# One core, Trainium2: the output product's first two loads issued 16 steps sooner, odd blocks' norms in later steps, the last pair's splits farther apart

## The chip, the cores and the metric

The kernel runs on one core of a Trainium2 chip. The metric is the time of one execution on the device, in microseconds (us), as the median of several runs.

## The reference

Attention in chunks gives `x` of 3072 tokens by 512; two mixtures follow it, each a small feed-forward net, with a norm between them:

```python
def _moe_ref(x, w_in, w_out):                 # 512 -> 2048 -> 512
    h = x @ w_in
    sp = np.where(h > 20.0, h, np.log1p(np.exp(np.minimum(h, 20.0))))
    g = h * np.tanh(sp)
    return (g @ w_out).astype(np.float32)

def _moe2_ref(x, w_gate, w_val, w_out, rms_g):  # 512 -> 1536 -> 512
    rms = np.sqrt(np.mean(x * x, axis=-1, keepdims=True) + 1e-06)
    xn = x / rms * rms_g
    g = xn @ w_gate
    silu = g * (1.0 / (1.0 + np.exp(-g)))
    val = xn @ w_val
    return (silu * val @ w_out).astype(np.float32)

x = attn_out.transpose(0, 2, 1, 3).reshape(3072, 512)
return _moe2_ref(_moe_ref(x, ...), ...)
```

## The kernel before, in words

All matrix work is done on TensorE (PE) in a split form: each fp32 operand is kept as hi + lo, and a product is three matmuls, hi by hi, hi by lo and lo by hi (`L639` to `L641` in `product`, `L754` to `L756` in `mm3`). The split is made by `split` (`L151` to `L154`): ScalarE (ACT) casts hi (`L153`), VectorE (DVE) subtracts to get lo (`L154`). POOL is GpSimd, SP is SyncE, which issues nearly all DMAs.

The stages in order of time:

- Attention, with the first products of the first mixture in its gaps, to about 300 us.
- `group1`: `x` by `w_in`, in groups of seven products (`group`, `L643` to `L670`) in place of eight. ScalarE copies a bank out (`L649`, `L657`), VectorE adds the rest (`L654`, `L665`, `L668`, `L670`). The result `g` goes to DRAM (`g_scratch`). The last pass, `group1(3, ...)`, ends at about 378 us.
- The output product of the first mixture, `out1`, 48 steps `(m, i)`: six blocks `m` of 512 tokens, eight steps `i` in each; a step is 24 matmuls. The class `Feed` loads the operand of a step from `g_scratch` (`L771`), applies mish (`L782`) and splits it. Three steps are prepared by `feeding` during the last group of the first mixture; later ones three to five steps ahead. This is the stage from about 378 to 640 us.
- The norm of a block, `rms_pieces`, is cut into pieces that wait in a list, `pend`; after a step of the next block a number of them, given by a tuple by `i`, are taken off and issued. Piece `p1` splits the sum of squares and adds it over the partitions with two matmuls by ones (`L833`); `p2` loads ScalarE's tables and takes the root by `Ln` and `Exp` (`L839` to `L841`). After an odd block the seven operands of the block pair are formed and split in the same way and stored to `nt_scratch`; a pair's seven operands are later loaded by `t_load` (`L628`), in the order 1, 6, 5, 4, 2, 7, 3.
- `group2`: the gated stage, for three pairs `j`, forwards and then backwards, from about 640 to 985 us. The last pair's operands are split while pair 0 is worked on: `both` puts the pieces in `pend`, an `x` of a string is a piece and a dot is an empty slot, and `between2` takes one off in each gap between products. When `pend` is empty `between2` goes on with the conversion of the weights (`L149` loads them raw, `L202` to `L216` convert).
- `group3`: the second output product, to the end.

The order of instructions is not that of the code alone. The program is given in the code's order and a scheduler then orders each engine's list, with the code's order as priority. So each engine works off a fixed list and stands where an instruction of it waits, with all behind it.

Of the kernel before, what the change touches and what calls it, by code (L numbers as in the profile page):

```python
# [29 lines left out]
def tile_kernel(  # L30
# [76 lines left out]
    def flush(all_=False):  # L107
        tick[0] += 1
        while late and (all_ or late[0][0] <= tick[0]):
            _, dst, src = late.pop(0)  # L110
            nc.sync.dma_start(out=dst, in_=src)


    def w_slot(u):
        pool = w1p if u < NW1 else w2p[0]
        return pool.tile([128, SLOT], F32R, tag=f"w{u}", name="w")
# [3 lines left out]
    def as7(s):  # L120
        return s.rearrange("p (a l f) -> p a l f", a=7, l=2)

    def w_load(key, u, cuts=((0, 7),)):
        s = w_slot(u)
        for a, b in cuts:
            at = slice(512 * a, 512 * b)
            nc.sync.dma_start(out=s[:, at].bitcast(F32), in_=wd[key][:, at].bitcast(F32))
        wtab[key] = as7(s)
# [180 lines left out]
    def cv_upto(n):  # L309
        while cv_n[0] < n:  # L310
            next(cv[0], None)
            cv_n[0] += 1
# [231 lines left out]
    def att_list(j):  # L544

        out = []
        t0 = TPP * j
        for s in range(TPP + 4):
            for op, lag in (("e", 4), ("d", 3), ("c", 2), ("b", 1), ("a", 0)):
                t = t0 + s - lag  # L550
                if t0 <= t < t0 + TPP:
                    if op == "a" and t % SPB == 0:
                        out.append([(att_a0, t)])
                    out.append([(att_ops[op], t), (att_ops[op + "1"], t)])
        return out
# [10 lines left out]
    def t_new2():  # L566
        return late_pools["t"].tile([128, 2, 2, N2], F32R, tag="T", name="T")
# [131 lines left out]
    def run(parts, between):  # L699
        while parts:  # L700
            for part in list(parts):
                if next(part, "end") == "end":
                    parts.remove(part)
                else:
                    between()
# [8 lines left out]
    def group1(j, i, between):  # L714
        run([group1_parts(j, i)], between)

    def group1_parts(j, i):
        need(("i", i))
        g = [gp.tile([128, 2, N], F32, tag="g", name="g") for _ in range(2)]
        ts = {p: ttab_x[j, p] for p in ORDER}  # L720
        at = W_AT if i < 3 else W_IN
        mul = lambda p, bank_, first: product(at[p], wtab["i", i], ts[p], bank_, first)
        banks = group_banks(4)
        c11 = banks[0][:, 0:N]
        temps = lambda: [cp.tile([128, N], F32, tag="c", name="c") for _ in range(3)]
        yield from group(mul, banks, N, g[0][:, 1, :], g[1][:, 0, :], g[1][:, 1, :], temps)
        nc.scalar.copy(g[0][:, 0, :], c11)
        for e in range(2):
            store_later(
                g_d[2 * i + e, :, 2 * N * j:2 * N * j + 2 * N].rearrange("p (a n) -> p a n", a=2),  # L730
                g[e],
            )
# [205 lines left out]
    down = up[::-1]  # L938
# [51 lines left out]
    def slots(pieces, conv, tail=(), more={}, cap=10 ** 6):  # L990


        state = dict(n=0, att=0, tail=0)
        plist, n_slots = pieces
        first_cv, to = conv
        base = cv_n[0]

        def between():
            state["n"] += 1
            n = state["n"]  # L1000
            flush()
            if n in more:
                more[n]()
            span = n_slots - 7
            while state["att"] < len(plist) and state["att"] * span < n * len(plist):
                for fn, t in plist[state["att"]]:
                    fn(t)
                state["att"] += 1
            if n > first_cv:
                cv_upto(min(cap, base + (to - base) * (n - first_cv) // (n_slots - first_cv)))  # L1010
            if n >= n_slots - 7 and tail:
                if state["tail"] == 0:
                    state["t"] = tail()
                    for fn in state["t"][0]:
                        fn()
                elif state["tail"] <= len(state["t"][1]):
                    state["t"][1][state["tail"] - 1]()
                state["tail"] += 1

        return between  # L1020

    def tail_of(j):
        return lambda: t_pieces(j, xb.pop(2 * j), xb.pop(2 * j + 1), t_new, lambda p: g_new(), None, ttab_x)
# [8 lines left out]
    CV_I = 64  # L1032
# [15 lines left out]
    more = {}  # L1048
    finish_at(more, 7, at[1, 7] + 1)
    bt = slots((att_list(1), 4 * len(units)), (0, 73), tail_of(1), calls(more), CV_I)  # L1050
# [4 lines left out]
    more = {}  # L1055
# [7 lines left out]
    bt = slots((att_list(2), 56), (12, CV_I + 33 + 11), tail_of(2), calls(more), CV_I + 33)  # L1063
    for i in down:
        group1(1, i, bt)
    more = {}
# [3 lines left out]
    bt = slots((att_list(3), 56), (0, 0), tail_of(3), calls(more))  # L1070
# [8 lines left out]
    w2p[0] = late_pool("w2p", 1, "right")  # L1079
    late_pools["s"] = late_pool("gs", 3, "right")  # L1080
    late_pools["gr"] = late_pool("gr", 1, "right")
    bt = slots(([], 56), (0, CV_I + 44))
    for pos, i in enumerate(down[:-1]):
        group1(3, i, bt)
        if 1 <= pos <= 3:
            back, u = ((1, 4), (2, 0), (0, 1))[pos - 1]
            w_load(("i", back), u)
    steps = [(m, i) for m in range(NB2) for i in range(F1 // 2)]

    def g_src(m, i):  # L1090
# [1 line left out]

    jorder = list(range(NPAIR2))
    feed = Feed(steps, g_src, ACTF.Mish)

    def feeding(feed, between):

        calls = [lambda: feed.load(4), lambda: None, lambda: feed.split(1), lambda: None,
                 lambda: feed.split(2), lambda: None, lambda: feed.split(3)]

        def fn():
            between()
            calls.pop(0)()

        return fn
# [8 lines left out]
    pend = []  # L1114
# [12 lines left out]
    for s, (m, i) in enumerate(steps):  # L1127
        t = feed.next(s)
        out1(m, i, t)
        flush()  # L1130
        if i == F1 // 2 - 1 and m < NB2 - 1:
            assert not pend
            p0, pend = rms_pieces(m, m, t_new2, sq_new, v_parts)
            p0()
            if m % 2:
                def both(m=m):
                    early, rest = t_pieces(m // 2, xn.pop(m - 1), xn.pop(m), t_new2, v_temp,
                                           nt_d[m // 2], {})
                    pend.extend(early + rest)
                pend.append(both)  # L1140
        elif i < F1 // 2 - 1:
            for _ in range((0, 1, 2, 2, 2, 3, 3)[i]):
                if pend:
                    pend.pop(0)()
        cv_upto(CV_I + min(64 + 78 * (s + 1) // len(steps), 44 + 4 * (s + 1)))
        n_raw[0] = 2 * (F1 // 2) + 6 + F1 + 12
        if m == NB2 - 1 and i in (1, 3, 5, 6):
            row_slots.clear()
            f, u = {1: (2, 5), 3: (3, 6), 5: (4, 3), 6: (5, 2)}[i]
            w_load(("gv", f), u)  # L1150
        if s == len(steps) - 3:
            t_load(jorder[0], nt_d[jorder[0]], ttab_n)
# [2 lines left out]
    hold = w_slot(0)  # L1155
    upper = hold[:, 4 * N2:6 * N2].bitcast(F32).rearrange("p (a n) -> p a n", a=2)

    def raw_pair():
        flush(True)
        parts = [rawp.tile([128, 512, 2], I32, tag="raw", name="raw") for _ in range(2)]  # L1160
        return tuple(
            x.rearrange("p f t -> p (f t)").bitcast(F32R).rearrange("p (a n) -> p a n", a=2)
            for x in parts
        )

    def last_temp(p):
# [5 lines left out]
    p0, pend = rms_pieces(  # L1172
        NB2 - 1, NB2 - 1,
        lambda: hold[:, 0:4 * N2].rearrange("p (a b n) -> p a b n", a=2, b=2),
        lambda: [upper[:, a] for a in range(2)], sm_parts, "1.2..rab",
    )
    p0()

    def both():
        early, rest = t_pieces(NPAIR2 - 1, xn.pop(NB2 - 2), xn.pop(NB2 - 1), raw_pair,  # L1180
                               last_temp, nt_d[NPAIR2 - 1], {})
        parts = early + rest
        pend.extend(parts.pop(0) if c == "x" else (lambda: None) for c in "x.x.x.xx.xxx")
    pend.append(both)

    def between2(to, n_slots):
        state = dict(n=0)
        base = cv_n[0]

        def fn():  # L1190
            flush()
            if pend:
                pend.pop(0)()
                return
            n_raw[0] = 10 ** 6
            state["n"] += 1
            cv_upto(min(to, base + (to - base) * state["n"] // n_slots))

        return fn

    bt = between2(CV_I + 220, 100)
    for jn, j in enumerate(jorder):
        last = jn == NPAIR2 - 1
        if jn:
# [28 lines left out]
    bt = between2(CV_I + 298, 92)  # L1233
# [54 lines left out]
```

## Time and profile before

| | before |
|---|---|
| runs, us | 1164.95, 1170.21, 1170.44 |
| median, us | 1170.21 |
| profiled execution, us | 1167.72 |
| its span, us | 1166.0 |
| mean granted clock of TensorE | 0.993 |

The profile is of one execution; its span runs from the first to the last instruction, and 1.7 us lie around it. A row of a timeline gives the start and the duration in us, the engine, the line of the code, the operation with its tiles, and in brackets how long the engine stood idle before it and what ended that. SPq is SyncE's queue of DMA issues; a row there gives the time the queue spent on issuing, not the transfer. Durations of neighbouring instructions on one engine overlap by about 0.1 us, so the time one takes in a row of them is read from start to start.

### The profile page before, as it was taken

How to read it: one execution, taken by the hardware profiler on the slowest of the kernel's cores; microseconds unless marked ns; L12 is line 12 of the kernel's file. 1: busy time of each engine (PE TensorE's matmuls, PEld its weight loads, DVE VectorE, ACT ScalarE, POOL GpSimd, SP SyncE). 2: the span in 40 equal slices, each digit the busy share in tenths (PEclk: the TensorE clock that was granted, in tenths of full speed). 3: DMA queues.
4: the chain of work that ended last, by engine and by line, in shares of the span. 5: the costliest groups of instructions: out<-in, count | busy, mean ns of one | idle time of the engine just before them, and what ended most of it. 6: DMA issues, size and time to landing. Idle time of an engine off the chain costs nothing.

```text
span 1166.0 us, 22910 instructions
## 1 busy us (share of the span) xinstructions
PE 1140.7 (98%) x9052; PEld 1005.2 (86%) x9052; DVE 823.8 (71%) x1254; ACT 629.2 (54%) x1008; POOL 183.4 (16%) x165
## 2 busy tenths in 40 slices
PE   5899999999999999999999999999999999999998
PEld 4799999999999888888878778888888888999998
DVE  3655798844745876866776765967896857888873
ACT  4566666543645896677775443544454423444441
POOL 3011231311132311010011121110211111000000
PEclk8899999999999999999999999999999999999999
DMA  9989799898488774594599398999898889655421
GB/s 195 187 219 224 191 300 260 240 297 284 170 302 290 255 225 144 188 354 157 195 375 409 123 349 316 355 407 359 312 363 356 329 283 319 180 160 145 145 91 37
DMA packets 213276, 294.20 MB, mean 252 GB/s; under 512 B 104240, under 2 KB 160560, under 8 KB 204336
## 3 DMA queue, kind: packets, MB, share of 16 engines
q1 hardware_dynamic: 210864, 284.34, 73.5%
q0 software_dynamic: 2304, 8.39, 2.3%
q8 instruction: 71, 1.16, 0.4%
q14 instruction: 37, 0.30, 0.1%
HBM read 181.80 MB, written 110.89 MB: 251 GB/s over the span
## 4 chain that ended last, share of the span: by engine, by line
PE 75%; DMA 9%; DVE 8%; ACT 5%; issue 2%; POOL 0%; SPq 0%; ACTq 0%; DVEq 0%; POOLq 0%
PE bk L639 13%; PE bk L640 13%; PE bk L641 13%; DMA s<-g_scratch 4%; PE bk L912 4%; PE bk L914 4%; PE bk L913 4%; PE bk L755 3%; PE bk L756 3%; PE bk L754 3%; DVE T L154 2%; PE bkp L639 2%; PE bkp L640 2%; PE bkp L641 2%; PE bkp L506 2%
## 5 line engine op out<-in xcount | busy, mean ns | idle before, releaser
L639 PE MATMUL bk<-T,w 128*128 128x384 f32 (+1 forms) x860 | 315.6, 369 | 1.3 <-ACT c L657 1.0
L640 PE MATMUL bk<-T,w 128*128 128x384 f32 (+1 forms) x860 | 311.2, 362 | 0.0
L641 PE MATMUL bk<-T,w 128*128 128x384 f32 (+1 forms) x860 | 307.4, 361 | 0.0
L639 PEld LDWEIGHTS bk<-T,w 128*128 128x128 f32 x860 | 162.0, 189 | 21.0 <-ACT c L657 1.3
L640 PEld LDWEIGHTS bk<-T,w 128*128 128x128 f32 x860 | 161.9, 188 | 16.5 <-DVE T L154 0.3
L641 PEld LDWEIGHTS bk<-T,w 128*128 128x128 f32 x860 | 161.5, 188 | 15.8
L912 PE MATMUL bk<-w,T 128*128 128x256 f32 x396 | 112.1, 283 | 0.2 <-ACT T L153 0.2
L913 PE MATMUL bk<-w,T 128*128 128x256 f32 x396 | 112.0, 283 | 0.0
L914 PE MATMUL bk<-w,T 128*128 128x256 f32 x396 | 111.9, 283 | 0.0
L755 PE MATMUL bk<-T,w 128*128 128x512 f32 x276 | 107.5, 390 | 0.5 <-DVE T L154 0.5
L756 PE MATMUL bk<-T,w 128*128 128x512 f32 x276 | 107.1, 389 | 0.0
L754 PE MATMUL bk<-T,w 128*128 128x512 f32 x276 | 105.8, 389 | 0.0
L669 POOL TENSOR_TENSOR v<-c,v 128x512 f32<-128x512 f32 x36 | 54.1, 1503 | 291.7 <-DVE c L665 259.0
L665 DVE TENSOR_TENSOR c<-bk,c 128x512 f32<-128x512 f32 (+2 forms) x72 | 43.0, 598 | 54.5 <-PE bk L641 41.9
L912 PEld LDWEIGHTS bk<-w,T 128*128 128x128 f32 x396 | 76.0, 192 | 0.5 <-ACT T L153 0.4
L913 PEld LDWEIGHTS bk<-w,T 128*128 128x128 f32 x396 | 76.0, 192 | 0.0
L914 PEld LDWEIGHTS bk<-w,T 128*128 128x128 f32 x396 | 75.9, 192 | 0.0
L649 ACT COPY c<-bk 128x512 f32<-128x512 f32 (+2 forms) x72 | 36.9, 514 | 69.1 <-PE bk L641 25.3
L154 DVE TENSOR_TENSOR T<-s,T 128x1024 fp32r<-128x1024 f32 (+1 forms) x50 | 62.5, 1258 | 15.2 <-ACT T L153 15.1
L782 ACT ACTIVATE s<-s 128x1024 f32<-128x1024 f32 x44 | 46.4, 1059 | 31.3 <-DMA s<-g_scratch 31.2
L755 PEld LDWEIGHTS bk<-T,w 128*128 128x128 f32 x276 | 51.8, 188 | 11.6 <-DVE T L154 0.9
L756 PEld LDWEIGHTS bk<-T,w 128*128 128x128 f32 x276 | 51.8, 188 | 10.8
(228 smaller groups left out, 2284.6 us busy)
## 6 DMA issues: line engine op xcount, KB each, us to landing
T<-nt_scratch SPq DMA_DIRECT2D x35, 1024.0 KB
g_scratch<-g SPq DMA_DIRECT2D x64, 384.0 KB
s<-g_scratch SPq DMA_DIRECT2D x46, 512.0 KB
h_scratch<-s SPq DMA_DIRECT2D x36, 512.0 KB
w<-wg SPq DMA_DIRECT2D x10, 1792.0 KB
wg<-w SPq DMA_DIRECT2D x30, 512.0 KB
raw<-in_moe_w_out_dram SPq DMA_DIRECT2D x28, 512.0 KB
nt_scratch<-T SPq DMA_DIRECT2D x14, 1024.0 KB
```

The source lines that it names most:

```text
L154: keep((eng or nc.vector).tensor_tensor(lo, src, hi.bitcast(F32), op=ALU.subtract))
L639: nc.tensor.matmul(ps, whi, xh, start=first and kk == 0, stop=False, **more)
L640: nc.tensor.matmul(ps, whi, xl, start=False, stop=False, **more)
L641: nc.tensor.matmul(ps, wlo, xh, start=False, stop=kk == 1, **more)
L669: nc.gpsimd.tensor_tensor(c22, u3, z5, op=ALU.add)
L754: nc.tensor.matmul(ps, ahi, bhi, start=start, stop=False)
L755: nc.tensor.matmul(ps, ahi, blo, start=False, stop=False)
L756: nc.tensor.matmul(ps, alo, bhi, start=False, stop=stop)
L782: nc.scalar.activation(x, g, self.act)
L912: nc.tensor.matmul(ps, t[:, 0, f], w[:, 0], start=first and f == 0, stop=False, **more)
L913: nc.tensor.matmul(ps, t[:, 0, f], w[:, 1], start=False, stop=False, **more)
L914: nc.tensor.matmul(ps, t[:, 1, f], w[:, 0], start=False, stop=f == HG - 1, **more)
```

## The change

Three parts. First, `feed.load(2)` is called in slot 40 of the last `group1` pass, and the definitions that it needs stand ahead of it; the splits of `feeding` come one slot sooner each. Second, in odd blocks the pieces in `pend` are taken off in later steps. Third, the string for the last pair's pieces has more dots, the fifth pair of tiles from `raw_pair` is a `T` tile in place of two raw ones, and the conversions of the weights are spread over 97 slots in place of 100.

```diff
--- before.py
+++ after.py
@@ -1079,24 +1079,23 @@
     w2p[0] = late_pool("w2p", 1, "right")
     late_pools["s"] = late_pool("gs", 3, "right")
     late_pools["gr"] = late_pool("gr", 1, "right")
-    bt = slots(([], 56), (0, CV_I + 44))
+    steps = [(m, i) for m in range(NB2) for i in range(F1 // 2)]
+
+    def g_src(m, i):
+        return g_d[2 * i:2 * i + 2, :, N2 * m:N2 * m + N2].rearrange("f p n -> p f n")
+
+    jorder = list(range(NPAIR2))
+    feed = Feed(steps, g_src, ACTF.Mish)
+    bt = slots(([], 56), (0, CV_I + 44), more={40: lambda: feed.load(2)})
     for pos, i in enumerate(down[:-1]):
         group1(3, i, bt)
         if 1 <= pos <= 3:
             back, u = ((1, 4), (2, 0), (0, 1))[pos - 1]
             w_load(("i", back), u)
-    steps = [(m, i) for m in range(NB2) for i in range(F1 // 2)]
-
-    def g_src(m, i):
-        return g_d[2 * i:2 * i + 2, :, N2 * m:N2 * m + N2].rearrange("f p n -> p f n")
-
-    jorder = list(range(NPAIR2))
-    feed = Feed(steps, g_src, ACTF.Mish)
-
     def feeding(feed, between):
 
-        calls = [lambda: feed.load(4), lambda: None, lambda: feed.split(1), lambda: None,
-                 lambda: feed.split(2), lambda: None, lambda: feed.split(3)]
+        calls = [lambda: feed.load(4), lambda: feed.split(1), lambda: None,
+                 lambda: feed.split(2), lambda: None, lambda: feed.split(3), lambda: None]
 
         def fn():
             between()
@@ -1139,7 +1138,7 @@
                     pend.extend(early + rest)
                 pend.append(both)
         elif i < F1 // 2 - 1:
-            for _ in range((0, 1, 2, 2, 2, 3, 3)[i]):
+            for _ in range(((0, 0, 1, 1, 1, 1, 0) if m % 2 else (0, 1, 2, 2, 2, 3, 3))[i]):
                 if pend:
                     pend.pop(0)()
         cv_upto(CV_I + min(64 + 78 * (s + 1) // len(steps), 44 + 4 * (s + 1)))
@@ -1155,8 +1154,14 @@
     hold = w_slot(0)
     upper = hold[:, 4 * N2:6 * N2].bitcast(F32).rearrange("p (a n) -> p a n", a=2)
 
+    raw_n = [0]
+
     def raw_pair():
         flush(True)
+        raw_n[0] += 1
+        if raw_n[0] == 5:
+            t = t_new2()
+            return t[:, 0], t[:, 1]
         parts = [rawp.tile([128, 512, 2], I32, tag="raw", name="raw") for _ in range(2)]
         return tuple(
             x.rearrange("p f t -> p (f t)").bitcast(F32R).rearrange("p (a n) -> p a n", a=2)
@@ -1180,7 +1185,7 @@
         early, rest = t_pieces(NPAIR2 - 1, xn.pop(NB2 - 2), xn.pop(NB2 - 1), raw_pair,
                                last_temp, nt_d[NPAIR2 - 1], {})
         parts = early + rest
-        pend.extend(parts.pop(0) if c == "x" else (lambda: None) for c in "x.x.x.xx.xxx")
+        pend.extend(parts.pop(0) if c == "x" else (lambda: None) for c in "x.x.x.x..xx.x.x")
     pend.append(both)
 
     def between2(to, n_slots):
@@ -1198,7 +1203,7 @@
 
         return fn
 
-    bt = between2(CV_I + 220, 100)
+    bt = between2(CV_I + 220, 97)
     for jn, j in enumerate(jorder):
         last = jn == NPAIR2 - 1
         if jn:
```

On ScalarE, at the end of the last `group1` pass and the start of the output product (`ca` and `lr` belong to the conversion of weights, `w<-sm` is hi of the third step's operand). Before:

```order
L649 COPY c<-bk_82 128x384
L202 ACTIVATE ca<-raw 128x512
L727 COPY g<-bk_82 128x384
L782 ACTIVATE sm<-w 128x1024
L657 COPY c<-bk_84 128x384
L153 CAST w<-sm 128x1024
L153 CAST w<-ca 128x512
L205 ACTIVATE lr<-raw 128x512
```

and now:

```order
L649 COPY c<-bk_82 128x384
L727 COPY g<-bk_82 128x384
L782 ACTIVATE sm<-w 128x1024
L657 COPY c<-bk_84 128x384
L202 ACTIVATE ca<-raw 128x512
L153 CAST w<-ca 128x512
L205 ACTIVATE lr<-raw 128x512
L153 CAST w<-sm 128x1024
```

One `L202` has gone from ahead of `L727` to behind the second `L657`, and with a cast of weights and an `L205` it now stands ahead of the `w<-sm` cast, which stood directly behind `L657`.

On VectorE in the same place (`L154 w<-sm` is lo of the same operand). Before:

```order
L209 TENSOR_SCALAR ca<-ca 128x512 x2
L654 TENSOR_TENSOR c<-bk_83,c 128x384
L210 SCALAR_TENSOR_TENSOR ca<-raw,ca 128x512 x2
L216 ISA ca<-ca,lr 128x1024
L665 TENSOR_TENSOR c<-bk_83,c 128x384
L154 TENSOR_TENSOR w<-sm,w 128x1024
L668 TENSOR_TENSOR g<-bk_84,c 128x384
L670 SCALAR_TENSOR_TENSOR g<-bk_85,c 128x384
L216 ISA ca<-ca,lr 128x1024
```

and now:

```order
L209 TENSOR_SCALAR ca<-ca 128x512
L654 TENSOR_TENSOR c<-bk_83,c 128x384
L210 SCALAR_TENSOR_TENSOR ca<-raw,ca 128x512
L216 ISA ca<-ca,lr 128x1024
L209 TENSOR_SCALAR ca<-ca 128x512
L665 TENSOR_TENSOR c<-bk_83,c 128x384
L210 SCALAR_TENSOR_TENSOR ca<-raw,ca 128x512
L668 TENSOR_TENSOR g<-bk_84,c 128x384
L670 SCALAR_TENSOR_TENSOR g<-bk_85,c 128x384
L216 ISA ca<-ca,lr 128x1024
L154 TENSOR_TENSOR w<-sm,w 128x1024
```

`L154 w<-sm` stood behind the first `L216` and `L665`; now the second `L209` and `L210`, `L668`, `L670` and the second `L216` stand ahead of it.

On TensorE, in the last odd block's stretch (`ones_r` are the norm's two matmuls). Before:

```order
L755 MATMUL bk_85<-T,w 128x512
L756 MATMUL bk_85<-T,w 128x512
L833 MATMUL bkp<-v,ones_r 128x512
L754 MATMUL bk_82<-T,w 128x512
L833 MATMUL bkp<-v,ones_r 128x512
L755 MATMUL bk_82<-T,w 128x512
L756 MATMUL bk_82<-T,w 128x512
```

and now:

```order
L754 MATMUL bk_85<-T,w 128x512
L755 MATMUL bk_85<-T,w 128x512
L756 MATMUL bk_85<-T,w 128x512
L833 MATMUL bkp<-v,ones_r 128x512 x2
L754 MATMUL bk_82<-T,w 128x512
L755 MATMUL bk_82<-T,w 128x512
L756 MATMUL bk_82<-T,w 128x512
```

The two norm matmuls stand together, and the first of them 24 matmuls later than before.

On SyncE, the second pair's seven loads (`T<-nt_scratch`) in the gated stage, with the stores of the last pair's operands (`nt_scratch<-`), of results (`h_scratch<-s`) and the raw weights (`L149`). Before:

```order
L628 DMA T<-nt_scratch 128x2048
L111 DMA h_scratch<-s 128x1024
L628 DMA T<-nt_scratch 128x2048
L111 DMA nt_scratch<-raw 128x1024
L628 DMA T<-nt_scratch 128x2048
L111 DMA nt_scratch<-raw 128x1024
L111 DMA h_scratch<-s 128x1024
L628 DMA T<-nt_scratch 128x2048 x2
L111 DMA nt_scratch<-raw 128x1024
L628 DMA T<-nt_scratch 128x2048
L111 DMA h_scratch<-s 128x1024
L628 DMA T<-nt_scratch 128x2048 x2
L111 DMA nt_scratch<-raw 128x1024
L111 DMA h_scratch<-s 128x1024
L111 DMA nt_scratch<-raw 128x1024
L149 DMA raw<-in_moe_w_gate_dram 128x4x256
```

and now:

```order
L111 DMA h_scratch<-s 128x1024
L111 DMA nt_scratch<-T 128x1024
L628 DMA T<-nt_scratch 128x2048
L111 DMA nt_scratch<-raw 128x1024 x2
L111 DMA nt_scratch<-T 128x1024
L628 DMA T<-nt_scratch 128x2048
L111 DMA h_scratch<-s 128x1024
L628 DMA T<-nt_scratch 128x2048 x2
L111 DMA nt_scratch<-raw 128x1024
L149 DMA raw<-in_moe_w_gate_dram 128x4x256
L628 DMA T<-nt_scratch 128x2048
L111 DMA h_scratch<-s 128x1024
L628 DMA T<-nt_scratch 128x2048 x3
L111 DMA h_scratch<-s 128x1024
```

Two stores from the `T` tile and a store of raw stand between and ahead of the first two loads, and the first weight load stands between the fourth and the fifth load; before it stood behind all seven and the next pair's first.

## Rows read from the trace of the kernel before

**Rows 1.** The page, section 1: busy time of TensorE, its share of the span, instructions.

```profile
PE 1140.7 (98%) x9052; PEld 1005.2 (86%) x9052; DVE 823.8 (71%) x1254; ACT 629.2 (54%) x1008; POOL 183.4 (16%) x165
```

**Rows 2.** Waits of PE from 300 to 700: total us, times, longest.

```profile
PE bkp L833 <- DVE v L154: 1.2, 1, 1.2
PE bk L639 <- ACT c L657: 1.0, 1, 1.0
PE bkp L639 <- DVE v L670: 0.9, 2, 0.7
```

**Rows 3.** Timeline of PE at 379: start, us, engine, line, operation, count, idle before, releaser.

```profile
378.98 0.40 PE L754 MATMUL bkp<-w 128*128 128x512 f32 x1
379.55 0.49 PE L755 MATMUL bk<-w 128*128 128x512 f32 x1 [0.17 <-DVE w L154]
```

**Rows 4.** Timeline of ACT (ScalarE) from 369 to 379.

```profile
369.66 0.66 ACT L202 ACTIVATE ca<-raw 128x512 f32<-128x512 f32 x1
370.23 0.66 ACT L205 ACTIVATE lr<-raw 128x512 int32<-128x512 uint32 x1
...
376.83 0.46 ACT L657 COPY c<-bk 128x384 f32<-128x384 f32 x1
377.19 1.05 ACT L153 CAST w<-sm 128x1024 fp32r<-128x1024 f32 x1
378.13 0.62 ACT L153 CAST w<-ca 128x512 fp32r<-128x512 f32 x1
378.65 0.67 ACT L205 ACTIVATE lr<-raw 128x512 int32<-128x512 uint32 x1
```

**Rows 5.** Timeline of DVE (VectorE) from 372 to 381.

```profile
372.15 0.78 DVE L209 TENSOR_SCALAR ca<-ca 128x512 int32<-128x512 int32 x2
372.85 0.55 DVE L654 TENSOR_TENSOR c<-bk,c 128x384 f32<-128x384 f32 x1
373.31 1.29 DVE L210 SCALAR_TENSOR_TENSOR ca<-raw,ca 128x512 int32<-128x512 int32 x2
374.51 0.69 DVE L216 CUSTOM_DVE_ANT_0 ca<-ca,lr 128x1024 uint16<-128x1024 uint16 x1
...
378.26 1.23 DVE L154 TENSOR_TENSOR w<-sm,w 128x1024 fp32r<-128x1024 f32 x1 [1.29 <-ACT w L153]
379.41 0.55 DVE L668 TENSOR_TENSOR g<-bk,c 128x384 f32<-128x384 f32 x1
379.88 0.55 DVE L670 SCALAR_TENSOR_TENSOR g<-bk,c 128x384 f32<-128x384 f32 x1
380.34 0.85 DVE L216 CUSTOM_DVE_ANT_0 ca<-ca,lr 128x1024 uint16<-128x1024 uint16 x1
```

**Rows 6.** Timeline of PE at the fifth block's norm.

```profile
600.00 0.39 PE L754 MATMUL bk<-T,w 128*128 128x512 f32 x1
601.55 0.50 PE L833 MATMUL bkp<-v,ones_r 128*128 128x512 f32 x1 [1.17 <-DVE v L154]
601.89 0.40 PE L755 MATMUL bk<-T,w 128*128 128x512 f32 x1
```

**Rows 7.** Timeline of SyncE's DMA queue (SPq), the second pair's operands.

```profile
678.93 0.38 SPq L628 DMA_DIRECT2D T<-nt_scratch  x1
...
681.73 0.32 SPq L628 DMA_DIRECT2D T<-nt_scratch  x1
...
684.40 0.32 SPq L111 DMA_DIRECT2D nt_scratch<-raw  x1
...
692.04 0.32 SPq L111 DMA_DIRECT2D nt_scratch<-raw  x1
```

**Rows 8.** Timeline of ACT: a cast that waits for a store.

```profile
694.69 1.05 ACT L153 CAST raw<-w 128x1024 fp32r<-128x1024 f32 x1 [2.79 <-DMA nt_scratch<-raw]
```

**Rows 9.** Timeline of DVE: a split that waits for a store.

```profile
702.41 1.23 DVE L154 TENSOR_TENSOR raw<-w,raw 128x1024 fp32r<-128x1024 f32 x1 [3.61 <-DMA nt_scratch<-raw]
```

**Rows 10.** Timeline of PE: operand 2 of the second pair, first matmul.

```profile
704.65 0.39 PE L639 MATMUL bk<-T,w 128*128 128x512 f32 x1
```

**Rows 11.** Table by stage, 675 to 715: busy us of each engine, PEclk, DMA share, GB/s.

```profile
675.00:715.00 40.00, 39.35 (x174) 32.24 (x173) 20.95 (x26) 12.02 (x19) 7.13 (x5) 1.00 0.90 357
```

## The prediction

> **What bounds the kernel now.** I read the page's busy line first, then the table of the waits, then the timelines of the engines at the places where the waits lie, and at last SyncE's timeline, from which transfer times follow. The busy line shows TensorE busy for 1140.7 of 1166.0 us [rows 1]. So the end is set by TensorE's matmuls, whose number the change leaves as it is, and what can be won or lost is TensorE's waiting. In the table of waits between 300 and 700 us the reader is to see how little that is: the longest entries are 1.2 us for a norm on VectorE's split, 1.0 us for ScalarE's copy and 0.9 us, in two waits, for VectorE's `v` [rows 2]. Ahead of 300 us the order is the same in both kernels. An edit can therefore win a few us at most; it can lose more, if it makes something late that is in time now. A measurement of this kernel tells about 0.5%, 5.85 us, from no change.
>
> The sum is made against the profiled execution's own time, 1167.72 us. That is 2.5 us below the median of the three runs, 1170.21, and between their ends, 1164.95 and 1170.44.
>
> **Part 1, the loads sixteen steps sooner.** The call stands sooner in the program, but SyncE's list of work has both loads at the same place as before, so the loads themselves gain or cost nothing. What the edit does move is the order of ScalarE and VectorE around 372 to 382 us, where the split of the output product's third step (`w<-sm`) is made. TensorE needs both halves: `L754` takes hi, `L755` takes hi and lo. In the trace of before `L755` started at 379.55, after 0.17 us of idle, as soon as VectorE's `L154` (378.26, 1.23 us) was done [rows 3, 5].
>
> On ScalarE `L657` (376.83) was followed by the cast at 377.19 [rows 4]. Now `L202 ca`, `L153 w<-ca` and `L205 lr` stand between. From start to start `L202` takes 0.57 (369.66 to 370.23), `L153` of this size 0.52 (378.13 to 378.65), and `L205` is taken like `L202`, 0.57: 1.66 us together [rows 4]. The hi half comes at about 379.9 in place of 378.2.
>
> On VectorE the lo half stood behind `L665` alone. Now the queue there is `L209`, `L665`, `L210`, `L668`, `L670`, `L216`, and then `L154`; the `L209` waits for the `L202` just named, which starts where the cast starts now (377.19) and takes 0.66, so ends at about 377.85. Start to start these take 0.35 (two `L209` from 372.15 to 372.85), 0.47 (`L668`, same size as `L665`: 379.41 to 379.88), 0.60 (two `L210` from 373.31 to 374.51), 0.47, 0.46 (`L670`, 379.88 to 380.34) and 0.69 (`L216`, 374.51): 3.04 us [rows 5]. `L154` then starts at 380.9 and ends, 1.23 later, at 382.15. TensorE's order of work has not moved there, so all its later matmuls stand behind `L755`, which starts at about 382.2 in place of 379.55: **+2.65 us**. The lower bound is 0 (the two queues meet TensorE no later than now); if ScalarE alone were late it would be 1.66.
>
> **Part 2, the norms of odd blocks.** The two `ones_r` matmuls of a norm go about 24 matmuls later in TensorE's order in blocks 1, 3 and 5. Blocks 1 and 3 show no wait there, so nothing is won. In block 5 the second of them waited 1.17 us for VectorE's `v`: between the starts of `L754` (600.00) and `L833` (601.55) lie 1.55 us where 0.22 is usual, and `L833` to `L755` takes 0.34, 0.11 over the usual [rows 6]. That is 1.33 + 0.11 = **-1.44 us**. Twenty-four matmuls at 0.227 give VectorE 5.4 us more, which covers a wait of 1.2. What is late next is the norm's scaling and the next pair's sums, 5.4 us later than now. The operands of the steps after it are split by VectorE too; they stand three steps of 5.45 us ahead, so the delay is one third of their lead, and I cost it at nothing. If that cover fails the wait is only moved: bound 0.
>
> **Part 3, the last pair's operand splits.** These fill the spaces of the first products of the gated stage and are stored to `nt_scratch`, while the seven operands of the second pair, 1 MB each (1024 KB), are loaded over the same queue. In SyncE's order the two stores that now come from a `T` tile, hi and lo, stand ahead of the first load and between the first two, and the first weight load (0.5 MB), which before stood behind all seven, now stands ahead of operand 2's. How fast the queue works is read from stores on which other engines waited. The store issued at 684.40 had landed when ScalarE went on at 694.69, the one issued at 692.04 when VectorE went on at 702.41 [rows 7 to 9]. Between them lay a store of `h` (0.5), two operands (2.0) and the second store itself (0.5): 3.0 MB in 7.72 us, 2.57 us per MB. The operand 1 load, issued at 678.93, has 3.5 MB between it and the first of these two landings, so it landed at about 694.69 - 3.5 x 2.57 = 685.7: 6.8 us after its issue.
>
> Now the `T` tile sits in the place of the first pair's operand 1, whose last readers stand, in TensorE's order, just ahead of one of the two waits for `v` [rows 2], ahead of the cast's turn on ScalarE; so the cast stops nobody. The second pair's operand 1 takes the place of operand 5, and its load goes at about 681.7, when in the trace of before the load of operand 6 went [rows 7]. It lands at 681.7 + 6.8 = 688.5. Behind it up to and with operand 2 stand three stores (1.5), operand 6, a store of `h` (0.5), operands 5 and 4, a store (0.5), the weights (0.5) and operand 2: 7.0 MB, 18.0 us, so operand 2 lands at 706.5. Its first matmul stands at the same place in TensorE's order as before, where it started at 704.65 [rows 10]. That is **+1.9 us**. Operand 7 (1.5 MB on, 710.4) is needed 18 matmuls after operand 2, at about 708.7, which the wait before it puts off to 710.6, and operand 3 likewise comes in time. Operands 6, 5 and 4, used 36, 24 and 12 matmuls of 0.227 us ahead of operand 2, come 0.4 to 1.6 us before that. The bounds: 0, if they all land in time; and the mean of the whole stretch, 357 GB/s, pauses included [rows 11], is 2.94 us per MB: operand 2 then lands at 709.1, 4.4 late, and operand 7 adds 0.4, together 4.8. I take 1.9, since the two landings are the nearest rows: the same kinds of transfers in the same places.
>
> The Trainium skill's page "DMA: Bandwidth & Descriptors", section "Where 436 GB/s comes from", says that transfers between HBM and SBUF are bound by the HBM side at about 358 GB/s per core, and that 435 is the ceiling of the ports. By an estimate from the first figure the third term would be 4.8 in place of 1.9 and the sum 1173.7. The stretch as a whole agrees (357); the 3.0 MB between the two landings went at 408 GB/s and speak against it as a limit.
>
> The rest of part 3, the weights' conversions about 14 us sooner and 97 slots in place of 100, is work of ScalarE and VectorE beside a TensorE that shows next to no waits there; I cost it at nothing. It costs what a late eviction costs, the 0.9 us of `v` [rows 2], if that cover is gone.
>
> **The sum**: 1167.72 + 2.65 - 1.44 + 1.9 = 1170.8 us. That is 0.6 over the median shown: no change that can be told.
>
> **Rivals.**
> (A) The second pair's operands land in time. For it: 2.3 us per MB would do, or an operand 1 that lands 1.9 us sooner, and they miss by 1.9 us in a chain of 25. Against it: the rate I took is already far above the stretch's mean. Sum 1167.72 + 1.2 = 1168.9.
> (B) Faster: the splits at 378 us come no later than now, and spreading the last pair's splits also lets `v` come in time, the 0.9 us of `v` [rows 2]. For it: VectorE has 1.29 us of idle time ahead of 378.26 [rows 5], into which work could fall. Against it: the order of both queues is fixed, and the split stands behind five more instructions. 1167.72 - 1.44 - 0.9 = 1165.4.
> (C) Slower: the queue goes at the stretch's mean in place of the rate between the landings, so operand 2 holds TensorE for 4.4 us and operand 7 for 0.4. Its place is the second pair's first products, at about 705 us. 1167.72 + 2.65 - 1.44 + 4.8 = 1173.7. It decides from 2.3 us per MB on, where operand 2 is first late; to be slower than the median by 0.5% it would take 3.2 us per MB (8.5 MB to operand 7, 7.1 us late). The skill's figure of 358 GB/s, above, stands for this rival.
> (D) Part 1 does what its words say and the loads do go sooner: no wait in the trace names them, so nothing follows.
>
> **How the numbers follow.** Forecast 0.5, A 0.2, B 0.1, C 0.15, and 0.05 for D and what I don't see. Predicted 1170.8. The cases lie between 1165.4 and 1173.7; runs of one kernel lie up to 2.8 us to either side of the profiled one. The range takes in half of that beside the lowest case and most of it beside the highest: 1164.2 to 1175.8. The lines of 0.5% about the median are 1164.4 and 1176.1. Faster by more takes B and a low set of runs: 0.04. Slower by more takes C and a high set, or a wait that I don't see: 0.07. Within: 0.89.
>
> **What would show it.** Part 1: `L755` behind the last group of the first product waits about 2.7 us more, for VectorE's `w L154`, at some 382 us. Part 2: the norm's 1.2 us is gone from the table of waits, and no `T L154` wait takes its place in the steps after. Part 3: a wait of `L639 bk` for the transfer `T<-nt_scratch` of 1.5 to 2.5 us at about 705 to 708, which is not there now. The prediction is wrong if TensorE waits nowhere at 382 (A's and B's side), or more than 5 us at 705, or at a place named nowhere above.

## The result: slower by 0.9%

The changed kernel takes 1177.92 us (median of 6 runs, 1174.66 to 1180.38), the kernel before 1167.26 (6 runs, 1164.9 to 1170.44). The ratio is 1.0088, with a 95% interval of 1.0063 to 1.0112. Predicted were 1170.8 us and no change that can be told; the measured median lies above the range. The profiled execution took 1174.66 us, the least of the six, 6.94 more than that of the kernel before (1167.72).

In the profile after, the busy time has hardly changed: TensorE is busy 1142.6 us where it was 1140.7 [rows 1]. The waits have. PE's waits from 300 to 720 us in the changed kernel, in us: total, times, longest, to be held against [rows 2] (`bk` and `bkp` are the banks that the matmuls write):

```profile
PE bk L639 <- DMA T<-nt_scratch: 2.9, 1, 2.9
PE bk L755 <- DVE w L154: 2.1, 1, 2.1
PE bk L754 <- ACT w L153: 1.3, 1, 1.3
PE bkp L639 <- DVE v L670: 1.0, 2, 0.8
PE bkp L639 <- DMA T<-nt_scratch: 0.7, 1, 0.7
PE bk L639 <- ACT c L657: 0.6, 1, 0.6
PE bk L755 <- DVE T L154: 0.6, 1, 0.6
```

The norm's `L833` is gone. New are `L754` and `L755` behind the third step's split, 3.4 us together where 0.2 stood, and two waits for the transfer `T<-nt_scratch`, 3.6 us. The wait for `T L154`, 0.6 us, was 0.5 before. The timeline of PE at the first of these places answers to [rows 3]:

```profile
377.36 0.33 PE L641 MATMUL bk<-T,w 128*128 128x384 f32 x1
378.96 0.73 PE L754 MATMUL bk<-w 128*128 128x512 f32 x2 [1.27 <-ACT w L153]
379.53 0.40 PE L754 MATMUL bkp<-w 128*128 128x512 f32 x1
382.02 0.76 PE L755 MATMUL bk<-w 128*128 128x512 f32 x1 [2.09 <-DVE w L154]
382.58 0.63 PE L756 MATMUL bk<-w 128*128 128x512 f32 x1
383.00 0.63 PE L755 MATMUL bk<-w 128*128 128x512 f32 x1
383.43 0.63 PE L756 MATMUL bk<-w 128*128 128x512 f32 x1
...
385.54 0.40 PE L756 MATMUL bkp<-w 128*128 128x512 f32 x1
385.77 0.40 PE L754 MATMUL bk<-w 128*128 128x512 f32 x1
```

In the kernel before the same `L641`, the last ahead of the third step, stood here:

```profile
378.33 0.34 PE L641 MATMUL bk<-T,w 128*128 128x384 f32 x1
```

So from it to `L755` it is 4.66 us (377.36 to 382.02) where it was 1.22 (378.33 to 379.55): 3.44 us more.

There is more here than the waits. After `L755` the matmuls of 512 columns start 0.427 us apart (382.58, 383.00, 383.43) and only from 385.54 on 0.227 again: half the rate. The table by stage of the changed kernel shows it as the granted clock (third number from the end, PEclk), which in the kernel before was 1.00 in each of these stretches:

```profile
370.00:385.00 15.00, 11.02 (x50) 9.32 (x49) 9.15 (x15) 8.70 (x14) 5.70 (x5) 0.90 0.78 258
385.00:400.00 15.00, 15.00 (x66) 12.36 (x66) 13.54 (x17) 13.63 (x19) 3.74 (x3) 0.98 0.69 239
400.00:420.00 20.00, 20.00 (x90) 16.56 (x89) 14.59 (x19) 14.21 (x21) 7.38 (x6) 1.00 0.59 189
```

The timelines of ACT and DVE answer to [rows 4] and [rows 5]. ACT:

```profile
375.87 0.46 ACT L657 COPY c<-bk 128x384 f32<-128x384 f32 x1
376.23 0.66 ACT L202 ACTIVATE ca<-raw 128x512 f32<-128x512 f32 x1
376.78 0.61 ACT L153 CAST w<-ca 128x512 fp32r<-128x512 f32 x1
377.30 0.68 ACT L205 ACTIVATE lr<-raw 128x512 int32<-128x512 uint32 x1
377.86 1.05 ACT L153 CAST w<-sm 128x1024 fp32r<-128x1024 f32 x1
```

DVE:

```profile
376.92 0.43 DVE L209 TENSOR_SCALAR ca<-ca 128x512 int32<-128x512 int32 x1 [3.20 <-ACT ca L202]
377.26 0.55 DVE L665 TENSOR_TENSOR c<-bk,c 128x384 f32<-128x384 f32 x1
377.73 1.57 DVE L210 SCALAR_TENSOR_TENSOR ca<-raw,ca 128x512 int32<-128x512 int32 x1
379.22 0.55 DVE L668 TENSOR_TENSOR g<-bk,c 128x384 f32<-128x384 f32 x1
...
380.75 1.21 DVE L154 TENSOR_TENSOR w<-sm,w 128x1024 fp32r<-128x1024 f32 x1
```

Both queues run as worked out, 0.96 us sooner as a whole (`L657` at 375.87, before at 376.83), but for `L210`, which took 1.49 us from start to start and not 0.60. POOL was at work beside it:

```profile
377.48 1.27 POOL L154 TENSOR_TENSOR w<-ca,w 128x512 fp32r<-128x512 f32 x1 [6.01 <-ACT w L153]
```

The second place, operand 2's first matmul, answers to [rows 10], and SyncE's rows to [rows 7]. PE:

```profile
702.88 0.50 PE L639 MATMUL bkp<-T,w 128*128 128x512 f32 x1 [0.65 <-DMA T<-nt_scratch]
...
708.23 0.39 PE L641 MATMUL bk<-T,w 128*128 128x512 f32 x1
711.47 0.50 PE L639 MATMUL bk<-T,w 128*128 128x512 f32 x1 [2.85 <-DMA T<-nt_scratch]
```

SPq:

```profile
684.69 0.43 SPq L628 DMA_DIRECT2D T<-nt_scratch  x1
...
696.12 0.43 SPq L149 DMA_DIRECT2D raw<-in_moe_w_gate_dram  x1
696.59 0.64 SPq L628 DMA_DIRECT2D T<-nt_scratch  x1
```

Operand 1's load goes at 684.69, the weights at 696.12, just ahead of operand 2's load, whose first matmul starts at 711.47 after 2.85 us of standing; the 0.65 us ahead of 702.88 are operand 4's.

To see where the time went in all, I summed over all matmuls of a trace how much later than usual the next one starts (usual is the median for its number of columns in the trace of the kernel before), by stage, in us. This counts waits and low clock together; spans differ by a little more, since some matmuls are not on record. The last three columns are kernels of the next section.

| stage, us | before | changed | changed, again (e9) | filled (e10) | e2 |
|---|---|---|---|---|---|
| 0 to 300 | 54.8 | 54.3 | 56.4 | 54.8 | 54.1 |
| 300 to 400 | 2.3 | 6.6 | 8.3 | 2.7 | 1.7 |
| 400 to 640 | 2.4 | 0.8 | -0.1 | -0.1 | 0.9 |
| 640 to 720 | 1.8 | 6.3 | 7.9 | 5.2 | 1.9 |
| 720 to the end | 0.8 | 0.3 | 1.7 | 0.6 | 0.0 |

So the profiled loss is +4.3 at 300 to 400, +4.5 at 640 to 720, -1.6 between them.

### The profile page after: what moved, and what is told of

It is laid out like the page before. It is cut to its first block, busy times and chain, and to the rows that moved or that the text cites. A ratio compares the mean times of both kernels' runs of the same rounds, so it can differ in the third digit from the quotient of the medians.

```text
span 1172.9 us, 22904 instructions
## 1 busy us (share of the span) xinstructions
PE 1142.6 (97%) x9052; PEld 1006.0 (86%) x9052; DVE 827.1 (71%) x1254; ACT 624.6 (53%) x1005; POOL 181.6 (15%) x165
## 4 chain that ended last, share of the span: by engine, by line
PE 76%; DMA 9%; DVE 7%; ACT 5%; issue 2%; SPq 0%; POOL 0%; ACTq 0%; POOLq 0%; DVEq 0%
PE bk L639 13%; PE bk L640 13%; PE bk L641 13%; PE bk L912 4%; PE bk L913 4%; PE bk L914 4%; PE bk L755 3%; PE bk L756 3%; PE bk L754 3%; DMA s<-g_scratch 2%; PE bkp L639 2%; PE bkp L640 2%; PE bkp L641 2%; DVE T L154 2%; ACT T L153 2%
## 5 line engine op out<-in xcount | busy, mean ns | idle before, releaser
L641 PE MATMUL bk<-T,w 128*128 128x384 f32 (+1 forms) x860 | 306.6, 361 | 0.0
L639 PEld LDWEIGHTS bk<-T,w 128*128 128x128 f32 x860 | 161.3, 188 | 23.6 <-DMA T<-nt_scratch 3.3
L640 PEld LDWEIGHTS bk<-T,w 128*128 128x128 f32 x860 | 161.7, 188 | 17.0 <-DVE T L154 0.6
L641 PEld LDWEIGHTS bk<-T,w 128*128 128x128 f32 x860 | 161.4, 188 | 15.7
L755 PE MATMUL bk<-T,w 128*128 128x512 f32 x276 | 107.5, 390 | 0.6 <-DVE T L154 0.6
L754 PE MATMUL bk<-T,w 128*128 128x512 f32 x276 | 106.3, 389 | 0.0
L665 DVE TENSOR_TENSOR c<-bk,c 128x512 f32<-128x512 f32 (+2 forms) x72 | 43.0, 597 | 57.7 <-PE bk L641 45.5
L154 DVE TENSOR_TENSOR T<-s,T 128x1024 fp32r<-128x1024 f32 (+1 forms) x50 | 62.5, 1258 | 24.5 <-ACT T L153 24.4
L755 PEld LDWEIGHTS bk<-T,w 128*128 128x128 f32 x276 | 51.8, 188 | 11.8 <-DVE T L154 1.1
L754 PEld LDWEIGHTS bk<-T,w 128*128 128x128 f32 x276 | 51.8, 188 | 10.9
L756 PEld LDWEIGHTS bk<-T,w 128*128 128x128 f32 x276 | 51.8, 188 | 10.7
```

The costliest lines, as they stand in the source:

```text
L154: keep((eng or nc.vector).tensor_tensor(lo, src, hi.bitcast(F32), op=ALU.subtract))
L639: nc.tensor.matmul(ps, whi, xh, start=first and kk == 0, stop=False, **more)
L640: nc.tensor.matmul(ps, whi, xl, start=False, stop=False, **more)
L641: nc.tensor.matmul(ps, wlo, xh, start=False, stop=kk == 1, **more)
L665: nc.vector.tensor_tensor(u3, y, s1, op=ALU.add)
L754: nc.tensor.matmul(ps, ahi, bhi, start=start, stop=False)
```

## The experiments

**e1, the calls alone.** The first part's two halves apart. In the built program the load at slot 40 alone leaves the order of every engine as it was, so only the list of calls can act; the load alone was not run. Up to 420 us the trace of e1 has the order of the changed kernel on every engine.

```diff
-        calls = [lambda: feed.load(4), lambda: None, lambda: feed.split(1), lambda: None,
-                 lambda: feed.split(2), lambda: None, lambda: feed.split(3)]
+        calls = [lambda: feed.load(4), lambda: feed.split(1), lambda: None,
+                 lambda: feed.split(2), lambda: None, lambda: feed.split(3), lambda: None]
```

> Of the three parts only the new list of calls in `feeding` (splits one slot sooner); the load at slot 40 is not made. My theory: the whole first place comes from this list, not from the load, and it costs two things: TensorE's waits for `w<-sm` at 378 to 382 us (3.1 us more waiting than in the kernel before) and a stretch at the lower granted clock right behind them, 1.5 us in the profiled execution of the changed kernel and more in others, since its other executions had a mean clock of 0.986 to 0.991 against 0.992. So 1171.5 to 1176 us where the kernel before has 1167.3, with a mean clock below 0.993 in most runs. Rival: the waits alone cost, and the lower clock in the changed kernel came from somewhere else (the 3 us wait at 708, say): then 1170.4 us and a clock of 0.993.

Measured: 1174.12 us, ratio 1.0068 (1.0052 to 1.0085). PE's waits at the place are 1.3 and 2.1 us as in the changed kernel, and the clock fell. Table by stage of e1:

```profile
370.00:385.00 15.00, 11.30 (x53) 9.72 (x52) 9.05 (x15) 8.99 (x14) 6.51 (x5) 0.86 0.80 272
385.00:400.00 15.00, 15.00 (x62) 12.27 (x61) 13.55 (x16) 13.62 (x19) 3.23 (x3) 0.91 0.72 234
```

So this list, and not the load, is the first place's cost; e11 below repeats it. It is not all of e1's time: a wait that neither the kernel before nor the changed one shows stands far behind, at 886 us, and in e11 there are two of them, 2.0 and 0.6 us at 881 and 888. The list moves some rows there too, on ScalarE, VectorE and SyncE at 887 to 927 us; e5, with the same list, shows no such wait.

```profile
886.26 0.47 PE L639 MATMUL bk<-T,w 128*128 128x512 f32 x1 [1.33 <-DMA T<-nt_scratch]
```

**e2, the norms alone.** `for _ in range(((0, 0, 1, 1, 1, 1, 0) if m % 2 else (0, 1, 2, 2, 2, 3, 3))[i]):` and nothing else.

> Only the norms of odd blocks in later steps. My theory: TensorE's wait of 1.44 us in the fifth block goes and nothing takes its place: 1165.6 us, ratio 0.9986, clock as before. Rival: the wait is moved to a later operand (as one of 0.6 to 1.4 us at `T L154`): 1167.3 us.

Measured: 1165.32 us, ratio 0.9988 (0.9977 to 0.9999): the second part is a gain, 1.4 us between the medians, and no wait came in its place (between 400 and 640 us the only one left is 0.4 us, in block 4). This is the best version of all.

**e3, the third part alone**, its three edits as in the diff of the change.

> Only the third part: the longer string, the `T` tile in place of the fifth pair of raw tiles, 97 slots. My theory: operand 2 of the second pair lands late, and operand 4 a little, 3.8 us of waiting together as in the changed kernel (0.8 and 3.0): 1171.2 us, ratio 1.0034, clock 0.993 as before. Rival: that wait, too, brings a stretch at the lower clock in some runs: 1173 us or more and a clock below 0.990 in them.

Measured: 1170.88 us, ratio 1.0049 (1.0028 to 1.0071). PE's waits of e3:

```profile
PE bk L639 <- DMA T<-nt_scratch: 1.9, 1, 1.9
...
PE bkp L639 <- DMA T<-nt_scratch: 0.9, 1, 0.9
```

The waits are there, 2.8 us, at a granted clock of 1.00 at this place.

**e4, second and third part**, the changed kernel without its first.

> The second and the third part together, so the changed kernel without its first part. My theory: the parts add up: 1167.3 - 1.6 + 3.8 = 1169.5 us, ratio 1.002, clock 0.993; the difference to the changed kernel (1177.9) of about 8 us is what the first part costs, waits and clock together. Rival, that the low clock needs the wait at 708 us and not the one at 380: some runs of this one at 0.986 to 0.990 and 1173 us.

Measured: 1170.65 us, ratio 1.0040 (1.0026 to 1.0054): within the intervals the second and third part add up. The first adds less well, though the intervals allow it: 1.0088 against 1.0040 leaves 0.0048 for it, and e1 alone cost 0.0068, with a wait at 886 us that the changed kernel does not have. Part of the rival came true as well: in this trace the clock fell at 706 us, behind the wait for operand 2 (0.91 from 700 to 720). So either place can bring it.

**e5, the calls with the second wait filled.** In `out1`, for the third step's first bank:

```diff
+                if (m, i, e, c) == (0, 2, 0, 0):
+                    pin(nc.tensor.matmul(ps, whi[:, s], t[0][:, e, :], start=False, stop=False))
+                    for _ in range(9):
+                        pin(nc.tensor.matmul(bk[0], whi[:, s], t[0][:, e, :], start=True, stop=True))
+                    pin(nc.tensor.matmul(ps, whi[:, s], t[1][:, e, :], start=False, stop=False))
+                    nc.tensor.matmul(ps, wlo[:, s], t[0][:, e, :], start=False, stop=False)
+                    continue
```

> As e1, with nine extra matmuls of 512 columns (2.04 us) in the second wait, between the first `L754` of the third step and the `L755` that waits for lo. They read hi, which is there, and write a bank that nobody reads before it is started anew, so the output is unchanged and VectorE's split ends no sooner or later. My theory: TensorE's standing is what lowers the clock, so with the second wait filled the granted clock stays 1.00 from 370 to 400 us (e1: 0.86 and 0.91), the matmuls behind it take 0.227 us from start to start in place of 0.427, and the kernel gains 2 to 3.5 us on e1: ratio to the kernel before about 1.003 to 1.0045 where e1 had 1.0068. Rival: the lower clock has to do with the place or with the first wait (1.4 us): the clock falls all the same, ratio 1.0068.

Measured: 1172.74 us, ratio 1.0047 (1.0029 to 1.0066). In the profiled execution, the shortest of the twelve (1168.05 to 1177.66 us), the clock stays up. Table by stage of e5:

```profile
370.00:385.00 15.00, 13.60 (x66) 11.41 (x65) 10.04 (x16) 9.40 (x14) 4.84 (x4) 1.00 0.71 246
385.00:400.00 15.00, 15.00 (x68) 12.43 (x67) 13.41 (x15) 13.40 (x18) 4.15 (x3) 1.00 0.78 250
```

The first wait (1.25 us) is still there and does not lower it. The interval overlaps e1's, so the time alone does not settle it; the trace shows it for one execution, and e10 for another. How often the clock stays up in the others is not shown.

**e6, the weights behind the operands.** As e3, and a flag that holds back the raw weights, and with them their conversions, until the second pair's loads are in the program:

```diff
+    hold_raw = [True]
...
+            if hold_raw[0]:
+                return
             n_raw[0] = 10 ** 6
...
             t_load(j, nt_d[j], ttab_n)
+            hold_raw[0] = False
```

> As e3, but the first raw weight load of the gated stage may not be issued before the second pair's loads are in the program, so it stands behind operands 2, 7 and 3 on the queue and not ahead of operand 2. My theory: the half MB of weights is 1.4 us of the wait for operand 2: in the trace that wait is 0.7 us in place of 2.1, that for operand 4 stays at about 1.0, ratio 1.0037 in place of 1.0049. Rival: the wait comes from the stores of the `T` tile and the later load of operand 1 alone (the queue has a pause where the weights went): 2.1 us stays.

Measured: 1169.83 us, ratio 1.0025 (1.0010 to 1.0039). PE's waits of e6:

```profile
PE bkp L639 <- DMA T<-nt_scratch: 0.8, 1, 0.8
...
PE bk L639 <- DMA T<-nt_scratch: 0.5, 1, 0.5
```

Operand 2's wait is 1.4 us shorter, operand 4's as before: the half MB of weights is that much of it. What is left, 1.3 us, was not taken apart by a run.

**e7, the `T` tile alone**, with the string and the 100 slots of the kernel before.

> Only the `T` tile for the fifth pair of raw tiles; the string of pieces and the 100 slots as before. My theory: the dots do nothing for the order of the transfers and the `T` tile does it all, so the waits for operands 4 and 2 are those of e3, 1.0 and 2.1 us, ratio 1.003 to 1.005. Rival: the string's dots put the stores ahead of the loads: then no such wait and ratio 1.000.

Measured: 1173.03 us, ratio 1.0055 (1.0033 to 1.0076), waits of 2.0 and 0.7 us for `T<-nt_scratch`. The third part's cost is the tile; that the string's dots do nothing against it is e3, at a ratio whose interval holds e7's.

**e8, the norms of even blocks too**: `(0, 0, 2, 3, 2, 3, 3)` for even `m`.

> As e2, and in even blocks the pieces taken off by 0, 0, 2, 3, 2, 3, 3 in place of 0, 1, 2, 2, 2, 3, 3, so that the norm matmuls move there too. My theory: the wait of `L833` for ScalarE's `v` in block 4 (0.3 to 0.6 us) goes, and nothing else: 0.5 us faster than e2, ratio 0.9983, the best version so far. Rival: the operands of the pair, which hang on the same list, come later and the 0.6 us wait for `T L154` behind them grows: ratio 0.999 to 1.001.

Measured: 1168.13 us, ratio 1.0009 (0.9994 to 1.0023). The rival held: block 4's 0.4 us is gone, and behind it the wait for the operand has grown. PE's waits of e8:

```profile
PE bk L755 <- DVE T L154: 1.4, 1, 1.4
```

**e9, e10, e11, on one chip: the changed kernel again, the changed kernel filled, the calls again.** e10 is the changed kernel with e5's edit.

> The changed kernel once more, for a second trace of it beside the next two on the same chip. My theory: the sum of the parts' ratios, 1.0068 (e1) + 1.0040 (e4) - 1 = 1.0108, or 1.009 to 1.011, and in the trace the same three places: the wait at 378 to 382 (3.7 us in all), a stretch at the lower clock behind it, and the wait for operands 4 and 2 (about 3.3 us), with a stretch at the lower clock behind it in some executions. Rival: part of the difference is at a place that the first profiled execution did not show; then a wait of over 1 us that is in none of the traces so far stands in this one.

> The changed kernel with e5's nine extra matmuls in the second wait of the third step. My theory: no lower clock behind 382 us, 1.5 to 3 us less than e9 on the same chip: ratio 1.0065 to 1.009, and the low clock that is left stands at about 705 us if anywhere. Rival: the clock falls in any case, ratio as e9.

> e1 once more, on the chip of the filled kernel. My theory: a granted clock below 1.00 between 370 and 400 us again, and a ratio of 1.006 to 1.008, above that of the filled kernel e5 (1.0047) by what the clock costs. Rival: the clock stays at 1.00 in this trace, so that the stretch in e1 was chance, and the ratio is that of e5.

Measured: e9 1178.49 us, ratio 1.0090 (1.0070 to 1.0110); e10 1174.10, 1.0051 (1.0035 to 1.0068); e11 1175.10, 1.0054 (1.0036 to 1.0072). The trace of e9 is of an execution of 1180.49 us, the longest of its five; its table by stage shows the low clock at both places:

```profile
370.00:385.00 15.00, 11.06 (x59) 9.96 (x58) 9.67 (x16) 7.61 (x13) 5.79 (x5) 0.96 0.77 250
385.00:400.00 15.00, 15.00 (x56) 12.05 (x56) 12.00 (x14) 13.23 (x18) 3.57 (x3) 0.82 0.70 236
700.00:720.00 20.00, 16.48 (x63) 12.53 (x62) 5.78 (x9) 5.80 (x10) 1.29 (x1) 0.91 1.02 418
```

and that of e10, of the shortest of its nine (1171.17 us), at neither:

```profile
370.00:385.00 15.00, 13.39 (x66) 11.36 (x65) 9.44 (x15) 8.93 (x14) 5.85 (x5) 1.00 0.77 255
385.00:400.00 15.00, 15.00 (x68) 12.42 (x67) 13.59 (x16) 13.57 (x19) 3.91 (x3) 1.00 0.72 241
700.00:720.00 20.00, 18.00 (x78) 14.47 (x79) 6.56 (x10) 5.28 (x9) 2.59 (x2) 1.00 0.98 388
```

By the medians, nine matmuls of no use make the kernel 4.4 us faster, and every run of e10 (1171.17 to 1175.73) lies below every run of e9 (1176.55 to 1180.49). The two traces, ends of their sets, lie farther apart than that: 3.6 us at 300 to 400 us (8.3 against 2.7 and the 2.0 us that the nine take), which is the fill's, and 2.6 at 640 to 720, where in e9 the low clock cost 1.5 us and the transfer wait was 0.9 longer; that is not at the place of the edit. e11 has the low clock again (0.87 and 0.90 in those two stretches), so e1's was not chance; its ratio is below e1's and not clear of e5's, and both e1 and e11 hold the wait at 881 to 888 us, so how much of the time of e1 the clock is stays open to within 2 us.

## Why the prediction was wrong

- **What bounds the kernel**: right. Of the 6.94 us the table by stage has 6.1 as TensorE's standing or its clock.
- **Part 1, +2.65**: the mechanism right, the size not. The mover is the list of calls (e1), not the load. `L755` came 3.44 us later: the step that failed is `L210` at 0.60; it took 1.49. The rows that I took the 0.60 from had an idle POOL beside them; the new order puts POOL's `L154` there (377.48 to 378.75), and `L210` ended 0.55 us behind it, at 379.30. No run moved POOL's work alone, but the traces bear it out: in all thirteen, 94 `L210` start while a `TENSOR_TENSOR` of POOL is under way, and 93 of them end 0.55 to 0.66 us behind its end; the 822 with POOL idle take 0.67 to 0.70 us.
- **The clock**: the term that is missing. I priced each wait at its own length. Behind the waits of 1.3 and 2.1 us the matmuls ran for 2.6 us (first trace of the changed kernel) to 5.2 us (e9) at half the rate: 1.6 to 2.7 us more at this place, 1.5 at the second in e9. No row of the kernel before shows this after 100 us, and no wait there is above 1.2 us; I should have carried it as a rival with a price, from the low clock in the first 60 us of that trace. The fill takes 4.4 us off the median (e9, e10). Of these the traces show 2.7 as the clock at the first place; the rest is not taken apart. With the fill, and the change's other waits, all nine runs of e10 lie inside the range; without it five of the result's six lie above.
- **Part 2, -1.44**: right, place and size: -1.4 (e2), nothing in its place. The interval of e2 takes in 0.1 to 2.7 us, so the size rests on the trace (-1.5 at 400 to 640).
- **Part 3, +1.9**: place and cause right, the size not: TensorE stood 0.7 us for operand 4 and 2.9 for operand 2 in the changed kernel, 0.9 and 1.9 in e3. The step that failed is the 6.8 us for operand 1, and with it operand 4 at nothing. I take a transfer as landed at the last update of its semaphore in the trace. In the kernel before operand 1 landed 6.8 us after its issue, as worked out; in the seven traces with the `T` tile it took 7.5 to 7.9. A store of `h` and one of the `T` tile, 1 MB, go out in the 1.2 us ahead of it (683.50, 683.92); I counted the second in the order and gave it no time.
- **Part 3, the rate**: 2.57 us per MB (408 GB/s) held in four of six traces: from operand 1's landing to operand 2's the 7.0 MB took 18.0 to 18.1 us in e3, e4, e7 and e10. In the two traces of the changed kernel, which alone of these have the low clock at the first place too, they took 18.9 and 19.2, 2.70 and 2.74 per MB, 0.9 to 1.2 us more; why is open. From operand 1's issue (684.69) to operand 2's first matmul (711.47) it was 26.8 us, where I had 24.8; in e3 25.9, and without the half MB of weights 24.3 (680.64 to 704.94, e6), so that half MB cost 1.6. The mean of the stretch, rival C's end, 2.94, was in none of them. The Trainium skill's 358 GB/s in "DMA: Bandwidth & Descriptors", section "Where 436 GB/s comes from", which stood for C, is 2.93 us per MB; these transfers did not keep to it.
- **The rest of part 3**, at nothing: right as far as the runs tell; the intervals of e7 and e3 overlap, and the 97 slots were not run alone.
- **The rivals**: C came nearest, 1173.7 against the profiled 1174.66, by luck: its rate was not seen, and what brought the time there is `L210`, operand 1 and the clock. None had the clock.

## What to carry to other kernels

A wait of TensorE can cost more than its length: look whether the matmuls behind it start farther apart, and what a filler that keeps the array busy gives back. Price an instruction from a row with the same engines at work beside it: `L210` was priced with POOL idle and met a busy one. Read the order of every engine that a moved call shares, not only that of the thing moved: here a split issued one slot sooner in the program reached TensorE 3.4 us later. And a buffer set free is an invitation to the next load: the tile that took a store off one pool let half a MB of weights in ahead of an operand that had no slack.

## What the runs showed of the hardware

The granted clock of TensorE takes two levels, and what brings the lower one behind the first place is TensorE's standing: with waits of 1.3 and 1.6 to 2.1 us there the matmuls behind start 0.427 us apart (512 columns at 1.2 GHz) in place of 0.227, in all four traces that have both waits (the changed kernel's two, e1, e11). In e5 and e10 the second wait was filled, the 1.3 us stood alone, and the clock there stayed at 1.00. A wait of 1.9 to 2.9 us at the second place brings the lower level in some executions (e4, e7, e9) and not in others (e3, e10, the first of the changed kernel). The timeline of PE of e9 at the second place:

```profile
714.25 0.50 PE L639 MATMUL bk<-T,w 128*128 128x512 f32 x1 [2.87 <-DMA T<-nt_scratch]
...
714.86 0.63 PE L641 MATMUL bk<-T,w 128*128 128x512 f32 x1
715.28 0.63 PE L639 MATMUL bk<-T,w 128*128 128x512 f32 x1
...
718.23 0.39 PE L640 MATMUL bk<-T,w 128*128 128x512 f32 x1
718.46 0.39 PE L641 MATMUL bk<-T,w 128*128 128x512 f32 x1
```

The Trainium skill's page "TensorE: Matmul & The Clock Gate", section "What's actually happening", names the same two levels and ties them to how busy the engine has been; the trace agrees, with starts 0.427 and 0.227 us apart. How long the matmuls then run at the half rate differs from run to run (2.6 to 5.2 us here). That can be a part of why one kernel's runs lie 4 to 10 us apart, but how much of it is not shown: those of the kernel before, whose trace shows a granted clock of 1.00 from 60 us on, lie 5.5 us apart.

A VectorE instruction can be held up by GpSimd: `L210` takes at most 0.70 us with POOL idle and up to 1.78 us when it starts beside a `TENSOR_TENSOR` of POOL, 0.55 to 0.66 us from that one's end in 93 of 94 cases.
